# The parameter loads on ScalarE's queue, the skip blocks by one GpSimd selection, and another order of the work

## The chip, the cores and the metric

The kernel runs on one core of a Trainium2 chip. A core has five engines with their own instruction queues: TensorE (PE, matmuls and transposes, with the weight loads PEld beside it), VectorE (DVE), ScalarE (ACT), GpSimd (POOL) and SyncE (SP, which here only issues DMA transfers). Each engine works through its own list in order, and semaphores hold an instruction back until what it reads is written and what it overwrites is read. The metric is the device time of one execution in microseconds (us).

## The reference

Two independent halves over a sequence of S = 2048 rows and D = 1024 columns in bf16, side by side in the output.

- Half A: `kv = shift(k) * v`, where `shift(k)` sums four shifted copies of k, each times a row of `shift_k`; then a long convolution along the sequence with the kernel `ssm_k` (by FFT in the reference), plus `kv * ssm_D`, times q.
- Half B: a diagonal complex state space model. From `Lambda_re`, `Lambda_im` and `log_dt` follow the factors `Lam_bar = exp(dt * Lam)`; then, in each channel p,

```python
Bu = einsum("bld,pd->blp", x, B_bar)
h  = Lam_bar * h + Bu[:, t, :]          # for every t of the sequence
y  = 2 * real(einsum("blp,dp->bld", hseq, Cmat)) + x * Dskip
```

## The kernel before

**How it is staged.** Half B goes through the sequence in 16 chunks of 128 rows. For chunk i, `U.i.jp.jl` (L457) multiplies the transposed x with the transposed matrices BT (16 matmuls of 128 columns each, two for the real and the imaginary part); `ue` evicts the bank to the arena; `r1` and `r2` (L483, L496) rotate by the tables Z1, so that the complex recurrence becomes a real one; `sc` (L502) scans it along the time axis, once for the real and once for the imaginary part; `r3` and `r4` rotate back by Z2; `y` (chunks 0, 1, 2, 14 and 15, L513) or `yq` (the others, in quarters of the array, L526) multiplies by CT and adds the skip term, a matmul of x with the diagonal block `Dd[:, d, :]`; `ye` evicts, and `yst`, `ysp`, `ysg` or `ysh` store. `cy` copies the last state of a chunk to the next.

Half A does its convolution as a transform in two steps: `kvm`, `kva`, `kvb`, `kvc` (L582 to L603) build kv on DVE; `am` and `ae` transform it and `ast` stores it to DRAM; `hl`, `hT`, `hc`, `hm`, `he`, `hst` do the same with `ssm_k`; then for 16 pairs of frequencies `lh`, `lk`, `lw` load both and the constants, `sh` and `sk` do the second step, `she` and `ske` evict, `sw` or `swp` swap rows by DMA, `pr` (L712) multiplies on DVE, `sa`, `sae` and `vst` transform back and store; at the end `vl`, `a3`, `a3e`, `qm` and `ost` or `osp` finish the rows.

**What sets the order.** Everything is written out by hand. The string ORDER (L67) lists 1489 words; each is a task with its arguments, and the letters behind the colon choose arena units (a), PSUM banks (p), scan buffers (h) and weight slots (w). The loop at L773 emits the tasks in that order, so each engine's list is ORDER with the other engines' tasks left out. A tile that reuses an arena unit or a bank waits until its last reader is done. A name with a v at the end (`bcv`, `skev`, `a3ev`) is the same eviction on DVE instead of ACT.

**The start of half B.** `ld_par` (L270) loads five vectors of 1024 numbers into the 40 rows of praw; `par_T` transposes them on PE, `p32` casts them to f32 on DVE; `exp1`, `dve2`, `exp2`, `dve3` make dt, the radius and the angle; `sm_pre`, `tabA1`, `tabA2` reduce angles on DVE (small ones and a table of 1024 columns), `sin0`, `sin1`, `sin2` take the sines on ACT; `par_rest` makes factors from sin0's result; `eo`, `stt`, `z1`, `z2` make the rotation tables Z1 and Z2; `rta` fills the scan's factors. `bl.j.w` loads a block of B, `bT` transposes it on PE (L415), `bc` on ACT or `bcv` on DVE evicts it into BT. `cl`, `cT`, `cc` do the same for C, or `cx` by a transposing DMA. `ld_w`, `wb` and `wbe` load `shift_k`, broadcast it over the partitions by matmuls with a row of ones, and evict it into wbc, which every `kvm` reads whole. `kp` and `vp` load rows of k and v, `x` loads a transposed block of x by DMA.

**The skip blocks.** Dd holds eight diagonal 128x128 blocks with Dskip on the diagonal. `dd` (L365) makes them as eight products of the identity with a column of p32, on DVE (its other form, on ACT, isn't in ORDER).

**Queues.** `spd` (L205) issues on SP, `gpd` (L206) on POOL. SP issues the parameter loads, all loads of B, C, x, k, v, q and the intermediate arrays, `swp`, `ysp`, `ysh`, `osp`; POOL the stores `ast`, `hst`, `vst`, `yst`, `ysg`, `ost`, the swaps `sw` and four small loads. ACT issues no DMA before the change.

Of the kernel before, what the change touches and what calls it, by code (L numbers as in the profile page):

```python
# [67 lines left out]
ld_w:a22 wb.3:p3 ld_par wbe.3:a8 par_T:p4 wb.0:p5 wb.7:p1 p32 ld_F bl.1.0:a39 bl.0.1:a18 wb.5:p7 bl.6.0:a34 bl.4.1:a14  # L68
exp1 dve2 wbe.0 dve3 wb.6:p2 wb.4:p3 wb.2:p0 sm_pre wbe.7 bl.0.0:a27 wbe.5 x.0:a38 wb.1:p7 wbe.6 exp2 kp.1:a0 bl.1.1:a21
kp.0 x.1:a33 bT.0.1:p4 sin0 bc.0.1 wbe.2 tabA1:a47a49a42a12 tabA2 bT.4.1:p5 bl.3.0:a24 bl.5.1:a18 bl.2.1:a51 bl.4.0:a22  # L70
bl.6.1:a41 wbe.1 bT.1.0:p6 sin1 dd wbe.4 bc.1.0 bT.0.0:p1 bl.5.0:a36 sin2 par_rest bc.0.0 bT.6.0:p0 bT.1.1:p6 eo bcv.1.1
bc.4.1 bl.2.0:a28 U.0.0.0:p1 bT.5.1:p3 U.1.0.1:p6 kp.-1 kvm.3:a29 bT.4.0:p7 bc.4.0 U.1.0.0 bT.6.1:p4 bcv.6.0 bT.5.0:p2
bT.2.1:p0 U.0.0.1 bT.3.0:p7 bc.5.0 bc.2.1 bc.5.1 kva.3 kring U.1.2.0:p5 bl.3.1:a23 cl.0.0:a14 bT.2.0:p2 bT.3.1:p0
bl.7.1:a46 ue.1.0:a34 U.0.2.1:p6 bc.3.1 bc.2.0 U.0.2.0 U.1.2.1 cl.3.0:a37 bl.7.0:a26 cl.1.0:a25 bT.7.1:p2 kvb.3:a22
bT.7.0:p0 ue.0.0:a23 bc.6.1 kp.-2 x.3:a21 U.0.1.0:p3 bc.3.0 gz stt cl.2.0:a12 cT.0.0:p4 bc.7.0 bc.7.1 U.0.1.1 U.0.3.0:p0
kvm.1:a15 ue.1.2 vp.1:a27 U.0.3.1 U.3.2.0:p1 ue.0.1 U.3.0.0:p3 z1 kvm.2:a42 z2 ld_Q U.1.1.1:p2 ue.0.2 ue.0.3 x.2:a52
U.1.1.0 cl.3.1:a13 kva.1 cT.1.0:p7 cl.2.1:a32 kva.2 kvb.1:a14 kvb.2:a39 ue.1.1 kvm.0:a15 rta kvc.3 U.3.0.1 cx.6.0 kva.0
cc.1.0 am.3.1:p0p6 cl.1.1:a51 U.3.1.1:p2 ue.3.0:a44 ae.3.0.1:a19 cc.0.0 U.3.2.1 kvc.2 ue.3.2 am.3.0:p7p3 cT.3.1:p0
vp.0:a30 cc.3.1 cx.7.0 kvb.0:a29 U.3.1.0 ue.3.1 cT.1.1:p5 U.3.3.0:p4 r1.0:a46 ae.3.1.1 kvc.0 U.3.3.1 kp.2 am.2.1:p2p0
r2.0:h1 cc.1.1 ue.3.3 cl.0.1:a27 hl.0.1:a23 kvc.1 am.0.0:p5p6 ae.3.0.0 cT.2.1:p1 ae.2.1.1:a40 sc.0.0 hl.0.0 U.1.3.1:p4  # L80
ae.3.1.0 sc.0.1 U.1.3.0 am.0.1:p3p0 ae.0.1.0:a31 cc.2.1 ae.0.0.0 ae.0.0.1 ae.0.1.1 ae.2.0.1 cT.0.1:p7 U.2.0.1:p1
r1.3:a15 cc.0.1 ue.1.3 ast.0 U.2.0.0 am.1.1:p5p3 r3.0:a27 cx.5.0 U.2.3.0:p0 ae.1.0.1:a46 hl.1.0:a48 hl.1.1 ae.1.1.1
am.1.0:p7p6 ae.1.1.0 ae.1.0.0 cT.3.0:p5 cx.4.0 r2.3:h2 cx.5.1 r4.0 cx.7.1 hT.0.1:p4 ue.2.0:a36 cx.4.1 cc.3.0 hT.0.4:p2
cy.1:h0 kvm.4:a14 hT.0.6:p7 hc.0.1:a22 am.2.0:p1p3 r1.1:a27 ae.2.1.0 U.2.3.1 ue.2.3 U.2.2.0:p5 kva.4 hc.0.4:a42 U.2.2.1
cx.6.1 ue.2.2 U.2.1.0:p3 cT.2.0:p2 hc.0.6:a32 cc.2.0 ae.2.0.0 U.2.1.1 ast.3 r2.1 ue.2.1 hT.0.2:p5 hT.0.3:p7 ast.1
hc.0.3:a18 hm.0.6.1:p4p2 hT.0.7:p0 he.0.6.1.1:a43 y.0.0.0:p3 y.0.0.1 hm.0.4.0:p2p6 hdv.0 hc.0.7:a12 he.0.6.1.0
hm.0.7.0:p4p1 hT.0.5:p0 he.0.4.0.1:a29 ast.2 hdv.1 sc.1.0 hT.0.0:p7 he.0.4.0.0 hst.0.4.0 hc.0.2:a20 y.0.0.2
he.0.7.0.0:a50 y.0.0.3 hc.0.0:a13 hm.0.6.0:p4p2 ye.0.0:a19 hm.0.4.1:p5p7 y.0.1.0:p6 y.0.1.1 y.0.1.2 y.0.1.3 vp.2:a34
kvb.4:a31 he.0.6.0.0 sc.1.1 he.0.4.1.1 vp.3:a26 r1.2:a14 he.0.4.1.0 he.0.7.0.1 hst.0.7.0 r3.1:a46 hm.0.0.1:p1p5
hst.0.4.1 hc.0.5:a42 he.0.6.0.1 r4.1 hm.0.0.0:p2p3 he.0.0.1.0:a48 cy.2:h1 r2.2 hm.0.5.1:p7p0 ye.0.1 he.0.5.1.1:a23  # L90
he.0.5.1.0 kp.3 he.0.0.1.1 kvm.6:a38 he.0.0.0.0 y.1.1.0:p4 kvc.4 y.1.1.1 hst.0.6.0 hst.0.6.1 kp.4 kva.6 hst.0.5.1
hm.0.5.0:p6p0 he.0.5.0.0 kvm.5:a14 y.1.1.2 he.0.0.0.1 kvb.6:a25 he.0.5.0.1 y.1.1.3 hm.0.7.1:p2p7 ye.1.1:a28 he.0.7.1.0
kva.5 am.4.0:p1p6 y.1.0.0:p4 he.0.7.1.1 x.4:a32 hm.0.3.0:p2p3 ae.4.0.0:a29 hm.0.3.1:p5p0 hst.0.0.1 hst.0.0.0
he.0.3.1.0:a36 kvc.6 y.1.0.1 he.0.3.1.1 hst.0.5.0 kvb.5:a12 sc.2.1 ae.4.1.0 he.0.3.0.1 kvm.7:a13 y.1.0.2 am.4.1:p1p7
hl.3.0:a40 he.0.3.0.0 hm.0.1.0:p5p0 y.1.0.3 he.0.1.0.0:a38 am.6.1:p5p6 ae.4.1.1 U.4.3.1:p7 he.0.1.0.1 ae.6.0.1:a17
hl.2.1:a44 U.4.3.0 kvc.5 ae.6.1.1 am.6.0:p6p5 U.4.0.0:p2 ae.4.0.1 ue.4.3:a23 U.4.1.1:p3 ae.6.0.0 hm.0.2.0:p0p6 ae.6.1.0
ye.1.0 kva.7 hm.0.1.1:p5p7 sc.2.0 hm.0.2.1:p1p4 hst.0.7.1 hl.3.1 he.0.2.0.0:a34 U.4.1.0 he.0.1.1.0 hl.2.0 he.0.2.1.1
kvb.7:a31 ysp.0 U.4.0.1 r3.2:a48 hT.1.6:p5 he.0.1.1.1 ast.6 ast.4 he.0.2.1.0 hT.1.5:p4 r4.2 he.0.2.0.1 kvc.7 hT.1.4:p6
U.4.2.1:p1 ue.4.1 ue.4.0 hc.1.6:a22 hc.1.4:a19 am.5.1:p7p0 hT.1.3:p2 U.4.2.0 hc.1.5:a33 hT.1.7:p3 am.5.0:p6p4
ae.5.0.1:a15 yst.1 cy.3 y.2.1.0:p7 kp.5 hT.1.1:p5 hst.0.2.0 hd.2 y.2.1.1 ae.5.1.0 hdv.3 ae.5.0.0 hc.1.7:a30 ae.5.1.1  # L100
hst.0.2.1 hT.1.2:p4 y.2.0.0:p6 ue.4.2 hc.1.1:a14 sc.3.1 sc.3.0 hT.1.0:p0 y.2.0.1 am.7.0:p3p1 hc.1.3:a18 hst.0.1.0
r3.3:a40 hm.1.7.1:p5p2 hc.1.0:a34 ae.7.1.0:a27 he.1.7.1.1:a25 hst.0.3.0 y.2.1.2 ae.7.0.0 hst.0.3.1 am.7.1:p2p1 ast.5
y.2.0.2 kvm.8:a48 r4.3 y.2.0.3 he.1.7.1.0 ae.7.0.1 hc.1.2:a31 y.2.1.3 ye.2.0:a47 hm.1.4.1:p4p6 ae.7.1.1 kva.8
hm.1.7.0:p3p5 ye.2.1 yq.3.0:p1p0 hst.0.1.1 he.1.7.0.1 he.1.7.0.0 hm.1.4.0:p7p2 yst.2 he.1.4.1.0:a29 kvm.9:a39 lw.3:w1
kvb.8:a38 he.1.4.0.1 vp.4:a12 yq.3.1 yq.3.2 he.1.4.1.1 he.1.4.0.0 hm.1.3.0:p5p6 he.1.3.0.1:a15 hm.1.3.1:p3p4 he.1.3.1.0
hst.1.7.0 he.1.3.1.1 yq.3.3 hm.1.2.1:p7p6 x.6:a37 he.1.2.1.0:a19 kva.9 he.1.2.1.1 he.1.3.0.0 kvc.8 x.5:a36 lw.1:w2
kvb.9:a35 kvm.10:a47 U.6.1.0:p3 U.6.1.1 am.8.1:p6p7 ast.7 hst.1.7.1 r1.4:a40 kva.10 ae.8.1.1:a44 hst.1.4.1 ae.8.0.1
r2.4:h0 am.8.0:p5p2 ae.8.0.0 ae.8.1.0 hst.1.4.0 ue.6.1:a38 yq.3.4 yq.3.5 hm.1.2.0:p5p7 he.1.2.0.0 x.7:a27 kp.7
hm.1.5.1:p2p6 he.1.5.1.1:a51 he.1.5.1.0 hst.1.5.1 yq.3.6 yq.3.7 ye.3.1:a24 hm.1.5.0:p6p4 kvm.11:a28 he.1.2.0.1 hst.1.2.0
hm.1.0.1:p3p5 cy.4 he.1.5.0.0 kp.6 kvb.10:a33 U.5.1.1:p2 U.5.1.0 sc.4.0 U.6.3.0:p7 kva.11 sc.4.1 hst.1.3.1 ye.3.0  # L110
ue.5.1:a40 he.1.0.1.0:a17 U.5.3.1:p2 hm.1.0.0:p3p1 kvc.9 ast.8 he.1.5.0.1 hst.1.5.0 kvb.11:a46 hm.1.6.0:p0p6 he.1.0.0.0
he.1.0.0.1 he.1.6.0.1:a47 U.5.3.0 hst.1.2.1 hst.1.3.0 U.6.3.1 he.1.6.0.0 U.6.0.1:p1 hm.1.1.0:p6p0 ue.5.3 ysp.3
# [730 lines left out]
```

## Time and profile before

| what | value |
|---|---|
| median of three runs | 343.81 us (343.48 to 343.87) |
| profiled execution, first to last instruction | 343.2 us |
| PE busy | 329.5 us, 96% |
| DVE busy | 325.1 us, 95% |
| ACT busy | 273.5 us, 80% |
| POOL busy | 68.9 us, 20% |
| mean DMA rate over the span | 294 GB/s |
| mean granted TensorE clock | 0.996 |

The profile's own execution has a span of 343.2 us; around the span lies what the runs' times hold besides, so the two are set side by side here. Busy times are unions over an engine's instructions. A matmul's end is modelled, so a busy PE is not a PE at its peak: its records stretch when it has to wait. A DVE or ACT row is a duration, and neighbours in a full queue overlap a little, so that the distance between starts is what one costs. "Idle before" in brackets behind a row is how long the engine had nothing running and what ended that.

### The profile page before, as it was taken

Reading aid. Unit: us, or ns where it says so; the run is one execution under the profiler, and the core shown is the slowest. Engines: PE = TensorE matmul, PEld = TensorE weight load, DVE = VectorE, ACT = ScalarE, POOL = GpSimd, SP = SyncE. Lnnn points to the kernel's source line nnn. Section 1 sums busy time; section 2 is a strip of 40 time slices with the busy share of each in tenths; the row PEclk is TensorE's granted clock in tenths of the full one; section 3 lists DMA queues with packets and bytes.
Section 4 is the critical chain, followed back from the end, with each engine's and each line's share of the span. In section 5 each row is a group of like instructions: output and inputs, shape, how many; then the busy total and the mean of one; then the engine's idle time right before and its main releaser. Section 6 shows DMA issues by size and latency. Waiting matters only on the chain.

```text
span 343.2 us, 11813 instructions
## 1 busy us (share of the span) xinstructions
PE 329.5 (96%) x5086; PEld 230.2 (67%) x5105; DVE 325.1 (95%) x263; ACT 273.5 (80%) x519; POOL 68.9 (20%) x111
## 2 busy tenths in 40 slices
...
GB/s 177 352 351 208 315 281 283 155 318 365 368 269 198 264 263 295 233 261 343 313 353 282 270 339 212 369 272 311 280 314 276 216 326 378 327 335 284 375 346 274
DMA packets 62592, 100.83 MB, mean 294 GB/s; under 512 B 29422, under 2 KB 31614, under 8 KB 62540
## 3 DMA queue, kind: packets, MB, share of 16 engines
...
## 4 chain that ended last, share of the span: by engine, by line
PE 74%; ACT 15%; DMA 4%; issue 3%; DVE 3%; SPq 0%; POOL 0%; DVEq 0%; POOLq 0%
PE bank L464 25%; PE bank L538 19%; PE bank L520 10%; PE bank L754 4%; PE bank L688 4%; PE bank L726 4%; PE bank L608 2%; PE bank L657 2%; ACT BT L431 2%; ACT arena L614 2%; ACT arena L473 2%; ACT CT L439 2%; ACT arena L637 2%; DMA wslot<-a_c_W 1%; DMA arena<-arena 1%
## 5 line engine op out<-in xcount | busy, mean ns | idle before, releaser
L464 PEld LDWEIGHTS <-BT 128*128 128x128 bf16 x2048 | 117.8, 98 | 14.4 <-issue 9.9
L464 PE MATMUL bank<-arena,BT 128*128 128x128 bf16 x2048 | 125.4, 221 | 1.1 <-ACT BT L431 0.9
L538 PE MATMUL bank<-CT,gslot 64*64 64x512 bf16 x1408 | 86.6, 378 | 0.0
L504 DVE TENSOR_TENSOR_SCAN gslot<-rtab,gslot 128x1040 bf16<-128x1040 f32 x32 | 73.0, 2311 | 0.5
L538 PEld LDWEIGHTS <-gslot 64*64 64x64 bf16 x1408 | 36.9, 107 | 30.8 <-issue 1.9
L473 ACT CAST arena<-bank 128x512 bf16<-128x512 f32 x63 | 40.5, 660 | 13.8 <-PE bank L464 13.4
L614 ACT CAST arena<-bank 128x512 bf16<-128x512 f32 x64 | 37.2, 680 | 6.7 <-PE bank L608 4.0
L697 ACT CAST arena<-bank 128x512 bf16<-128x512 f32 x63 | 35.0, 617 | 5.9 <-issue 2.8
L520 PE MATMUL bank<-CT,gslot 128*128 128x512 bf16 x153 | 38.5, 380 | 0.3
L665 ACT CAST arena<-bank 128x512 bf16<-128x512 f32 x64 | 35.2, 631 | 3.1 <-PE bank L657 3.0
L714 DVE TENSOR_TENSOR arena<-arena 128x4096 bf16<-128x4096 bf16 x16 | 36.5, 2280 | 1.1 <-DMA arena<-arena 1.0
L487 DVE TENSOR_TENSOR arena<-gslot,Z 128x4096 bf16<-128x4096 bf16 x16 | 36.6, 2287 | 0.8 <-DVE gslot L504 0.2
L704 ACT CAST arena<-bank 128x512 bf16<-128x512 f32 x60 | 34.4, 621 | 3.2 <-PE bank L688 3.0
L734 ACT CAST arena<-bank 128x512 bf16<-128x512 f32 x60 | 32.4, 616 | 5.5 <-PE bank L726 5.3
L487 DVE TENSOR_TENSOR arena<-arena,Z 128x4096 bf16<-128x4096 bf16 x16 | 36.5, 2280 | 0.1
L556 ACT CAST arena<-bank 128x512 bf16<-128x512 f32 x31 | 18.1, 599 | 16.6 <-PE bank L538 8.7
L588 DVE TENSOR_TENSOR arena<-arena 128x4096 bf16<-128x4096 bf16 (+3 forms) x16 | 30.0, 1881 | 0.0
L668 POOL DMA_DIRECT2D Ys_h<-arena x32 | 23.2, 735 | 25.5 <-ACT arena L665 20.2
L617 POOL DMA_DIRECT2D Ys_kv<-arena x16 | 11.2, 726 | 83.5 <-ACT arena L614 81.1
L520 PEld LDWEIGHTS <-gslot 128*128 128x128 bf16 x160 | 14.1, 98 | 15.9 <-issue 2.3
L688 PE MATMUL bank<-arena,wslot 64*64 64x512 bf16 x256 | 21.5, 382 | 0.3 <-DMA wslot<-a_c_W 0.3
...
## 6 DMA issues: line engine op xcount, KB each, us to landing
...
```

The source lines that it names most:

```text
L464: nc.tensor.matmul(pu[:, w, jl, :], BT[:, 2 * jp + jl, w, d, :], xT[:, d, :], start=(d == 0), stop=(d == ND - 1))
L473: cp(st["u", i][:, :, 2 * jp:2 * jp + 2, :], st.pop(("pu", i, jp)))
L487: nc.vector.tensor_mul(m, s_, win(Z))
L504: nc.vector.tensor_tensor_scan(gf, rtab[:].rearrange("p j t -> p (j t)"), gf, 0.0, ALU.mult, ALU.add)
L520: nc.tensor.matmul(py, h[:, w, j, 2:GW], CT[:, j, w, dh * 512:(dh + 1) * 512], start=(j == 0 and w == 0), stop=False)
L538: mm = nc.tensor.matmul(st["py", i, dh][cols, cs(r)], lhs(dh, rows, c), rhs(dh, rows), start=first, stop=last)
L614: cp(st["ysb", n2][:, p, dh * 512:(dh + 1) * 512], st.pop(("pa", n2, p, dh)))
L665: cp(o, st.pop(("pb", hf, s, e, r)).rearrange("p (n c t) -> p n c t", n=2, c=2))
L688: nc.tensor.matmul(st["ps", nm, g, l][64 * dh:64 * dh + 64, :], st["w", i][rows, a * WC:a * WC + 64], st[nm, i][rows, a, dh * 512:(dh + 1) ...
L697: cp(st["hab", i][:, 0, a, l, :], st.pop(("ps", "h", g, l)))
L704: cp(st["x16", i][:, a, l, :], st.pop(("ps", "k", g, l)))
L714: nc.vector.tensor_mul(hab, st.pop(("x16", i)).rearrange("p a l d -> p (a l d)").unsqueeze(1).to_broadcast([P, 2, 2 * D]), hab)
```

## The change

Three edits. `ld_par` issues its five loads on ScalarE's queue instead of SyncE's. `dd` is one GpSimd selection over all eight blocks: the input is the eight columns of p32, each repeated 128 times along the free axis, and an element is kept where its column number equals its partition number and is 0 elsewhere. ORDER is a new list of the same 1489 tasks, but for the engine of some evictions and the queue of some stores.

```diff
 def ld_par():
     praw = const.tile([5 * NJ, P], BF16, name="praw")
     for pi, ap in enumerate((B_log_dt, B_Lre, B_Lim, B_Dskip, A_ssm_D)):
-        spd(praw[pi * NJ:(pi + 1) * NJ, :], ap.rearrange("(j i) -> j i", i=P))
+        nc.scalar.dma_start(praw[pi * NJ:(pi + 1) * NJ, :], ap.rearrange("(j i) -> j i", i=P))
...
-def dd_(act):
-    for d in range(ND):
-        skip = sm["p32"][:, 3 * NJ + d:3 * NJ + d + 1]
-        if act:
-            nc.scalar.activation(Dd[:, d, :], ident[:], ACT.Copy, scale=skip)
-        else:
-            nc.vector.tensor_scalar(Dd[:, d, :], ident[:], skip, None, ALU.mult)
-E["dd"] = lambda: dd_(False)
-E["dda"] = lambda: dd_(True)
+def dd():
+    skip = sm["p32"][:, 3 * NJ:3 * NJ + ND].unsqueeze(2).to_broadcast([P, ND, P])
+    nc.gpsimd.affine_select(out=Dd[:], in_=skip, pattern=[[0, ND], [-1, P]], compare_op=ALU.is_equal,
+                            fill=0.0, base=0, channel_multiplier=1)
+E["dd"] = dd
```

The lists of the single engines at the start, before (-) and after (+), taken out of ORDER:

```diff
 SP
-ld_par bl.1.0 bl.0.1 bl.6.0 bl.4.1 bl.0.0 x.0 kp.1 bl.1.1 kp.0 x.1 bl.3.0 bl.5.1 bl.2.1 bl.4.0 bl.6.1 bl.5.0 bl.2.0 kp.-1
+bl.1.0 bl.0.1 bl.6.0 bl.4.1 bl.0.0 x.0 kp.1 bl.1.1 kp.0 x.1 bl.3.0 bl.5.1 bl.2.1 bl.4.0 bl.6.1 bl.5.0 bl.2.0 kp.-1
 DVE
-p32 dve2 dve3 sm_pre tabA1 tabA2 dd par_rest bcv.1.1 kvm.3 bcv.6.0 kva.3 kvb.3:a22 stt kvm.1 kvm.2
+p32 dve2 dve3 tabA1 sm_pre tabA2 par_rest bcv.6.0 kvm.3 bcv.4.1 kva.3 bcv.1.1 kvb.3:a15 stt kvm.1 kvm.2
 ACT
-wbe.3 exp1 wbe.0 wbe.7 wbe.5 wbe.6 exp2 sin0 bc.0.1 wbe.2 wbe.1 sin1 wbe.4 bc.1.0 sin2 bc.0.0 eo bc.4.1 bc.4.0
+ld_par exp1 wbe.7 wbe.0 wbe.6 exp2 wbe.3 wbe.5 wbe.4 bc.0.1 bc.0.0 sin1 sin0 bc.1.0 wbe.2 wbe.1 sin2 eo bc.4.0
 PE
-wb.3 par_T wb.0 wb.7 wb.5 wb.6 wb.4 wb.2 wb.1 bT.0.1 bT.4.1 bT.1.0 bT.0.0 bT.6.0 bT.1.1 U.0.0.0
+par_T wb.7 wb.0 wb.6 wb.5 wb.3 wb.4 bT.0.1 bT.0.0 bT.1.0 bT.6.0 wb.2 wb.1 bT.4.1 U.0.0.0
 POOL
-ld_w ld_F kring gz ld_Q rta ast.0 ast.3 ast.1 ast.2 hst.0.4.0
+ld_w gz ld_F kring ld_Q rta ast.0 ast.3 ast.1 dd ast.2 hst.0.4.0
```

In DVE's list later on:

```diff
-r1.2 r3.1 r4.1 r2.2 kvm.6 kvc.4 kva.6
+r1.2 r3.1 kvc.4 r4.1 kvm.6 r2.2 kva.6
...
-r2.9 r1.10 sc.9.0 sc.9.1 r3.9 pr.6 r4.9 pr.8 r2.10
+r2.9 sc.9.1 sc.9.0 r3.9 r4.9 pr.6 r1.10 pr.8 r2.10
```

DVE has 22 evictions before (two of them `bcv`) and 21 after (three `bcv`). PE has the same matmuls; its list behind `yq.8.0` holds the same ones in another order, but for `sh.12` and `sh.13`, which now stand ahead of it. SP stores six whole y blocks (`ysp`) instead of seven, POOL eight (`yst`) instead of seven; of the last two chunks' halves SP stores three (`ysh`) instead of one, POOL one (`ysg`) instead of three; of the rows of half A SP stores five (`osp`) instead of four.

237 lines of the change are left out of this document (119 added, 118 removed).

## The prediction

> **What bounds the kernel now.** I read the stages first: the busy time of each engine between moments that matter to the change. In each row come the stretch (us), its length, then the busy time of PE, weight loads, DVE, ACT and POOL with the number of instructions.
>
> ```profile
> 4.48:20.72 16.24, 14.24 (x118) 11.57 (x118) 14.05 (x36) 16.21 (x35) 1.74 (x6) 1.00 1.09 344
> 20.72:37.95 17.23, 17.23 (x310) 17.16 (x308) 17.23 (x29) 16.43 (x22) 0.00 (x0) 1.00 1.24 275
> 37.95:71.72 33.77, 32.85 (x427) 25.70 (x434) 33.32 (x24) 33.24 (x54) 4.97 (x7) 1.00 0.92 266
> 71.72:208.03 136.31, 135.05 (x2167) 93.52 (x2180) 135.45 (x96) 115.89 (x228) 38.36 (x57) 1.00 0.94 291
> 208.03:325.40 117.37, 116.75 (x2013) 76.15 (x2017) 114.38 (x71) 84.97 (x172) 15.59 (x24) 1.00 0.96 308
> 325.40:343.20 17.80, 12.60 (x66) 5.82 (x63) 10.52 (x11) 5.37 (x10) 4.37 (x7) 0.93 0.86 313
> sum 343.20, PE 329.48 PEld 230.25 DVE 325.14 ACT 273.54 POOL 68.91; mean PE 47.07 PEld 32.89 DVE 46.45 ACT 39.08 POOL 9.84
> ```
>
> From 20.72 to 208 us DVE is idle for 0.45 us in the third row and 0.86 (136.31 - 135.45) in the fourth: it sets the pace, with ACT nearly as full up to 72 us. PE shows as full there too, but a matmul record stretches while PE waits, so that says less. From 208 us to 325.4 us PE is idle for 0.62 us and DVE for 2.99: there PE's work sets the pace, and DVE has slack. The span of this execution is 343.20 us, 0.61 below the 343.81 us median; I carry that 0.61 over.
>
> So a gain must make DVE reach 208 us earlier; what it then spares behind that point is slack. One of its waits in between stands in the list of waits (who waited for whom, us, times, longest):
>
> ```profile
> DVE gslot L498 <- PE bank L523: 0.4, 1, 0.4
> ```
>
> It is r2.2, which wants gslot 1 while the y matmuls of chunk 0 still read it. The other waits stand in brackets in DVE's own start, in order of time:
>
> ```profile
> 4.48 0.20 DVE L284 CAST p<-bank 128x40 f32<-128x40 bf16 x1 [3.48 <-PE bank L279]
> ...
> 6.90 1.17 DVE L320 TENSOR_TENSOR arena<-iot,thn 128x1024 f32<-128x1024 f32 x1
> ...
> 9.97 0.69 DVE L329 TENSOR_SCALAR arena<-arena 128x1024 f32<-128x1024 f32 x1
> ...
> 11.84 1.38 DVE L371 TENSOR_SCALAR Dd<-ident,p 128x128 bf16<-128x128 bf16 x8
> 13.14 0.17 DVE L336 TENSOR_TENSOR lb<-so,r 128x16 f32<-128x16 f32 x1
> ...
> 14.21 0.68 DVE L427 TENSOR_SCALAR BT<-bank 128x1024 bf16<-128x1024 bf16 x1
> 14.81 2.28 DVE L588 TENSOR_TENSOR arena<-arena 128x4096 bf16<-128x4096 bf16 x1
> 17.01 0.68 DVE L429 COPY BT<-bank 128x1024 bf16<-128x1024 bf16 x1
> 17.61 1.21 DVE L595 TENSOR_TENSOR arena<-arena 128x2048 bf16<-128x2048 bf16 x1
> 20.11 0.69 DVE L601 TENSOR_TENSOR arena<-arena 128x1024 bf16<-128x1024 bf16 x1 [1.28 <-PE bank L415]
> 20.72 0.34 DVE L354 SCALAR_TENSOR_TENSOR Z<-arena,b 128x128 bf16<-128x128 f32 x1
> ```
>
> The distance from one start to the next is what an instruction costs in a full queue: the eight products of dd 13.14 - 11.84 = 1.30 us, a BT eviction (bcv) 0.60, the four-block product (kvm) 2.20, a 1024-column sum 0.61. In front is the arrival of the parameters (3.48 us); at 20.11 a sum of the A half (kvb.3) has waited 1.28 us for a transpose (L415) that was still reading its arena unit.
>
> **The change, part by part.** *The five parameter loads.* SP issues them from 0.74 us on, and B's loads stand behind them:
>
> ```profile
> 0.74 0.42 SPq L273 DMA_DIRECT2D praw<-in_B_log_dt_dram  x1
> ...
> 2.23 0.30 SPq L273 DMA_DIRECT2D praw<-in_A_ssm_D_dram  x1
> 2.57 0.37 SPq L420 DMA_DIRECT2D arena<-in_B_B_re_dram  x1
> ```
>
> B's first load moves up by 2.57 - 0.74 = 1.83 us, and everything early on SP's queue with it. ACT starts at 0.73 us too, so the parameters need not land sooner. No row shows what an issue costs ACT. By SP's rows five end at 2.53 us and the table load of 1.28 us behind them at about 3.8, before the first exponential at 4.82: cost nothing. If ACT pays more, or loads its table first (1.28), everything on DVE starts up to 1.3 us later. The other bound is a gain of about 0.5, a broadcast's pace on ACT (4.33 to 4.82, below), since par_T no longer stands behind a broadcast matmul on PE. I take 0, as no row says that the loads had landed by then.
>
> *The order at the start.* tabA1 is moved ahead of sm_pre and tabA2 behind it: the same instructions, so DVE ends tabA2 at 11.84 us as before. dd is gone; par_rest follows, but it reads sin0, which the new order puts late on ACT. ACT's rows:
>
> ```profile
> 4.33 0.58 ACT L408 CAST arena<-bank 128x512 bf16<-128x512 f32 x1 [2.32 <-PE bank L402]
> 4.82 0.21 ACT L287 ACTIVATE dt<-p 128x8 bf16<-128x8 f32 x1
> 5.01 2.05 ACT L408 CAST arena<-bank 128x512 bf16<-128x512 f32 x4
> 6.92 0.24 ACT L293 ACTIVATE r<-a__130 128x8 f32<-128x8 f32 x1
> 7.18 1.28 ACT L314 ACT_TABLE_LOAD   x1
> ```
>
> New on ACT: six wbe from 5.01 us at 0.51 each, to 8.1; exp2, to 8.3; bc.0.1 and bc.0.0 at 0.95 (three took 2.85, below), to 10.2; the table load, to 11.5; sin1 about 1.0 (as many columns as a bc) and sin0 0.2, to 12.7. So par_rest starts at 12.7 us instead of 13.14: of dd's 1.30 us only 0.44 come off here, as ACT is late next. par_rest takes 14.21 - 13.14 = 1.07, to 13.8; bcv.6.0, to 14.4. kvm.3 reads all of wbc, whose last parts (bc.1.0, wbe.2, wbe.1: 0.95 + 2 x 0.51) ACT ends at 14.7, so it starts there, 0.1 before the 14.81 of now. Then 2.20 + 0.60 (bcv.4.1, taken over from ACT) + 1.21 + 0.60 + 0.61 leads to stt at 19.9 us instead of 20.72. The 1.28 us wait is gone, because kvb.3 now writes unit 15, which nothing used; a moved eviction takes 0.60 of it back. **DVE is 0.8 us earlier.**
>
> *Up to r1.0.* The first rotation starts at 37.95 us, where the second row above ends; DVE was full from 20.72 on. It also needs ACT's last ue of chunk 0:
>
> ```profile
> 21.89 2.85 ACT L431 ACTIVATE BT<-bank 128x1024 bf16<-128x1024 bf16 x3 [0.57 <-PE bank L415]
> ...
> 36.12 1.62 ACT L473 CAST arena<-bank 128x512 bf16<-128x512 f32 x3
> ```
>
> ue.0.3 is the second of the three in the last row: done at about 37.2 us. In the new order ACT has as many instructions ahead of this point (36; rta in, one bc out, both near 0.95 us). It loses the 0.49 us from 4.33 to 4.82, in which it evicted a broadcast while the parameters were under way, and may win back the 0.57 us it waited for a transpose, since B's blocks come earlier. So ACT is ready between 37.1 and 37.7 us, DVE at 37.1. I take 37.2: **0.75 gained**, with bounds of 0.25 and 1.2 (the whole 1.28 less what ACT holds).
>
> *r2.2.* In the new order kvc.4 and kvm.6 stand ahead of it (0.6 + 2.2 us of work that was due anyway) while the matmuls it waited for stay where they were in PE's order. The 0.4 us wait is covered: **0.4 gained**. For waits that I don't see in the new order I take 0, between another 1.3 lost (as long as the wait at 20.11) and the 0.86 of idle time left before 208 us gained.
>
> *dd on GpSimd.* The selection stands behind ast.1 on POOL. The nearest rows are the small selection that makes the identity and ast.1's store:
>
> ```profile
> 1.18 0.28 POOL masks.py:199 TENSOR_SCALAR_AFFINE_SELECT ident<-ident 128x128 bf16<-128x128 bf16 x1
> ...
> 53.78 0.69 POOL L617 DMA_DIRECT2D Ys_kv<-arena  x1 [2.43 <-DMA CT<-in_B_C_im_dram]
> ```
>
> Among Dd's readers the first y matmul comes at 62.2 us, and DVE meanwhile runs products of two inputs:
>
> ```profile
> L523 PE MATMUL bank<-Dd,arena x40: 218/219/220, 62.2 to 337.8; 128*128 128x128 bf16 x40
> ```
>
> ```profile
> 55.87 2.28 DVE L487 TENSOR_TENSOR arena<-arena,Z 128x4096 bf16<-128x4096 bf16 x1
> ```
>
> Eight times the columns cost between 0.3 us (if the 0.28 is all overhead) and 8 x 0.28 = 2.3. Behind ast.1 the selection would run from about 54.5 to 57 us, 5 us before the reader at 62.2; only ast.2's store is queued behind it. I take no cost. If it blocks DVE, up to 2.3 us comes on the pace: that is a rival.
>
> *The rest.* The compute order up to chunk 8 has the same DVE work per chunk, apart from neighbours exchanged. Behind it DVE gets two evictions fewer (2 x 0.60), and r4.9 comes 4.4 us of DVE work earlier (r1.10 and pr.6, about 2.2 each, now follow it): slack on an engine that doesn't set the pace there. y stores that change between SP and POOL move no work onto PE or DVE. PE's list behind yq.8.0 has the same matmuls but for sh.12 and sh.13, which now go just ahead of it, so its 117.37 + 17.80 us stay within some tenths.
>
> **Sum:** 0.75 + 0.4, about 1.2 us: span 342.0, time 342.0 + 0.61 = **342.6 us**.
>
> **The rivals.** (1) *Hidden anyway, by ACT.* r1.0 waits for ue.0 until 37.7 and another wait takes r2.2's place: 0.25 gained, 343.5 us. For it: ACT is idle for only 0.03 + 0.80 us between 4.48 and 37.95. Against it: B's loads come 1.83 us earlier. (2) *The search found more.* The 0.86 us of DVE idle before 208 us and the 0.62 of PE behind it go as well: 341.1 us; with r1.0's better bound 340.6. For it: r4.9 is ready longer before PE wants it. Against it: PE's 116.75 us behind 208 remain whatever the order. (3) *GpSimd's selection stops DVE, slower.* Should the selection hold up DVE's products between 54.5 and 57 us for its whole 2.3 us, the sum is 1.2 - 2.3: 344.9 us. It comes out slower from a price of 1.9 us on; at 1 us it only eats the gain. For it: DVE is full there, with two-input products such as the one at 55.87 us. Against it: beside a full DVE, POOL's work now is only DMA issues, and no row shows a DVE product held up. The Trainium skill (SBUF — State Buffer, "Who interferes with whom") states this as a rule: a DVE instruction with two SBUF inputs and a GpSimd instruction that reads SBUF exclude one another, and the second to issue blocks until the first ends. By that rule either DVE waits, as priced here, or the selection does, at no cost with its 5 us in hand; no run here shows which. (4) *The move of the parameter loads doesn't do what it says:* ACT issues them behind its table load or more slowly, all of DVE starts 1.3 us later and the sum is -0.1: 343.9 us.
>
> **How the numbers follow.** A difference under 0.2% (0.69 us) can't be told from none here. Forecast 0.40; (1) 0.21; (2) 0.19; (3) at its full price 0.14; (4) 0.06. Faster by over 0.2% (below 343.1): 0.40 + 0.19 = 0.59. Within 0.2%: 0.21 + 0.06 = 0.27. Slower: 0.14. Likeliest time 342.6; the range goes from (2) at its better bound to (3), 340.6 to 344.9.
>
> **What would show it.** Right: B's first load issued near 0.74 us, stt near 19.9, r1.0 near 37.2, no wait before r2.2, then yq.8.0 near 206.8 us with PE's stretch behind it unchanged in length. Wrong: the first cast of the parameters later than 4.5 us (4); a DVE product beside the selection much longer than 2.3 us, or a gap there (3); DVE idle before r1.0 on an ACT eviction (1); a shorter stretch behind yq.8.0 (2).

## The result, and the profile after

The changed kernel is slower: 349.22 us median of four runs (347.92 to 349.55) against 343.64 us (343.21 to 343.87) for the kernel before on the same chip, a ratio of 1.014 with an interval of 1.0109 to 1.0171. The forecast was 342.6 us, between 340.6 and 344.9: wrong in its sign, and outside its range.

The profiled execution of the changed kernel took 349.0 us and spans 347.3 us. Here are its stages, with the same columns as the rows of the kernel before: stretch, length, busy time of PE, weight loads, DVE, ACT and POOL.

```profile
0.00:6.01 6.01, 0.23 (x2) 0.21 (x3) 0.17 (x2) 1.28 (x1) 5.35 (x16) 1.00 0.64 218
6.01:21.28 15.27, 12.16 (x129) 9.11 (x129) 13.20 (x29) 14.87 (x32) 0.29 (x2) 1.00 1.09 330
...
76.27:212.11 135.84, 133.02 (x2140) 90.98 (x2139) 132.35 (x94) 113.97 (x224) 37.91 (x56) 1.00 0.90 286
212.11:325.80 113.69, 113.17 (x2010) 76.41 (x2008) 110.89 (x65) 83.32 (x170) 15.60 (x24) 1.00 0.93 308
325.80:347.30 21.50, 17.18 (x88) 7.92 (x86) 13.69 (x16) 7.23 (x13) 2.00 (x3) 0.98 0.81 303
```

The cuts are at the same instructions as before: the cast of the parameters (6.01 us, was 4.48), the first stt (21.28, was 20.72), r2.2 (76.27), the end of r4.8 (212.11), which in the kernel before lies within half a us of yq.8.0's start, and a late one. Two things are to be seen. The last two rows add up to 135.19 us; in the kernel before 343.2 - 207.59 = 135.61 us lay behind the end of r4.8. So nothing was lost there. And in the row from 76.27 to 212.11 DVE is idle for 135.84 - 132.35 = 3.49 us; it was 0.86 before. The time was lost ahead of r4.8's end, on DVE. DVE's rows of the changed kernel show where (in brackets the idle time ahead of a row and what ended it):

```profile
6.01 0.20 DVE L285 CAST p<-bank 128x40 f32<-128x40 bf16 x1 [4.94 <-PE bank L280]
...
14.26 0.18 DVE L337 TENSOR_TENSOR lb<-so,r 128x16 f32<-128x16 f32 x1 [1.16 <-ACT so L315]
...
20.68 0.68 DVE L598 TENSOR_TENSOR arena<-arena 128x1024 bf16<-128x1024 bf16 x1
...
38.68 2.29 DVE L484 TENSOR_TENSOR arena<-arena,Z 128x4096 bf16<-128x4096 bf16 x1
...
55.58 2.67 DVE L507 TENSOR_TENSOR gslot<-arena 128x2048 bf16<-128x2048 bf16 x1
...
76.27 1.22 DVE L495 TENSOR_TENSOR gslot<-arena 128x2048 bf16<-128x2048 bf16 x1
...
97.05 2.33 DVE L501 TENSOR_TENSOR_SCAN gslot<-rtab,gslot 128x1040 bf16<-128x1040 f32 x1 [0.31 <-ACT gslot L497]
...
146.08 0.69 DVE L600 TENSOR_TENSOR arena<-arena 128x1024 bf16<-128x1024 bf16 x1 [1.92 <-DMA arena<-in_A_v_dram]
...
201.94 2.32 DVE L501 TENSOR_TENSOR_SCAN gslot<-rtab,gslot 128x1040 bf16<-128x1040 f32 x1 [0.74 <-ACT gslot L497]
...
210.89 1.22 DVE L507 TENSOR_TENSOR gslot<-arena 128x2048 bf16<-128x2048 bf16 x1
```

The last row is r4.8. In the kernel before it stood here:

```profile
206.37 1.22 DVE L510 TENSOR_TENSOR gslot<-arena 128x2048 bf16<-128x2048 bf16 x1
```

So it comes 4.52 us later now, and the span is 4.1 us longer (347.3 against 343.2). In order:

- The parameters land late: the cast is at 6.01 instead of 4.48, and r1.0 (38.68) is 0.73 us later than before instead of 0.75 earlier.
- r4.0 (55.58) takes 2.67 us, where the same form takes 1.22 elsewhere: 1.45 lost, beside the selection.
- r2.2 (76.27) no longer waits: 0.4 won, as forecast.
- A product with v (kvc.13, 146.08) waits 1.92 us for v's rows; two scans wait 0.31 and 0.74 us for the copy of the state (cy) on ACT.

The losses add up to 0.73 + 1.45 + 1.92 + 0.31 + 0.74 - 0.4 = 4.75 us, against 4.52 measured at r4.8.

The 5.6 us between the medians are more than the 4.1 between the spans. The prediction set 0.61 us around the span of the kernel before. In the later runs, which list time and span of each execution, a run stands 1.6 to 2.2 us above its span with every kernel (349.0 against 347.3 here; 344.32 against 342.6 for one run of the kernel before). The time of the execution of the kernel before that was profiled is not on record; by this it took about 343.2 + 1.7 = 344.9 us (an estimate), about 1.1 above its median, so that the two traces show that much less than the medians. Single executions of one kernel lie up to about 2 us from its median and sometimes more; below, a time is judged by its ratio and interval, and a trace by the place where it loses time. The ratios leave out executions that took over 1.5% longer than the fastest of the same kernel (one each of f1 and f3 below, f3's at 855.65 us, and two of the kernel before), which the medians include, so that a ratio is not exactly the quotient of two medians.

### The profile page after: what moved, and what is told of

Its sections match the earlier page's. It is cut to its first block, busy times and chain, and to the rows that moved or that the text cites. A ratio compares the mean times of both kernels' runs of the same rounds, so it can differ in the third digit from the quotient of the medians.

```text
span 347.3 us, 11812 instructions
## 1 busy us (share of the span) xinstructions
PE 328.4 (95%) x5105; PEld 228.4 (66%) x5105; DVE 325.2 (94%) x254; ACT 273.6 (79%) x520; POOL 68.6 (20%) x110
## 4 chain that ended last, share of the span: by engine, by line
PE 47%; DMA 3%; DVE 1%; ACT 1%; issue 0%; SPq 0%; ACTq 0%
PE bank L535 18%; PE bank L461 13%; PE bank L723 4%; PE bank L751 4%; PE bank L517 4%; PE bank L685 4%; DMA arena<-Ys_kv 2%; DVE arena L484 1%; DMA wslot<-a_c_W 1%; ACT arena L731 0%; PE bank L520 0%; ACT arena L694 0%; ACT arena L553 0%; SPq L674 0%; ACTq L553 0%
## 5 line engine op out<-in xcount | busy, mean ns | idle before, releaser
L461 PEld LDWEIGHTS <-BT 128*128 128x128 bf16 x2048 | 116.6, 98 | 18.3 <-issue 12.2
L535 PE MATMUL bank<-CT,gslot 64*64 64x512 bf16 x1408 | 85.2, 377 | 0.3 <-ACT arena L694 0.2
L470 ACT CAST arena<-bank 128x512 bf16<-128x512 f32 x63 | 38.5, 629 | 10.0 <-PE bank L461 7.1
L611 ACT CAST arena<-bank 128x512 bf16<-128x512 f32 x64 | 35.7, 633 | 7.8 <-PE bank L605 4.5
L701 ACT CAST arena<-bank 128x512 bf16<-128x512 f32 x60 | 34.0, 631 | 8.4 <-PE bank L685 7.3
L694 ACT CAST arena<-bank 128x512 bf16<-128x512 f32 x62 | 34.7, 626 | 2.4 <-PE bank L685 2.2
L731 ACT CAST arena<-bank 128x512 bf16<-128x512 f32 x63 | 33.7, 629 | 2.4 <-PE bank L723 2.4
L662 ACT CAST arena<-bank 128x512 bf16<-128x512 f32 x64 | 34.0, 628 | 1.2 <-PE bank L654 1.2
L553 ACT CAST arena<-bank 128x512 bf16<-128x512 f32 x31 | 18.1, 612 | 18.4 <-PE bank L535 10.7
L758 ACT CAST arena<-bank 128x512 bf16<-128x512 f32 x23 | 12.6, 593 | 11.8 <-PE bank L751 11.7
```

The source lines that it names most:

```text
L461: nc.tensor.matmul(pu[:, w, jl, :], BT[:, 2 * jp + jl, w, d, :], xT[:, d, :], start=(d == 0), stop=(d == ND - 1))
L470: cp(st["u", i][:, :, 2 * jp:2 * jp + 2, :], st.pop(("pu", i, jp)))
L535: mm = nc.tensor.matmul(st["py", i, dh][cols, cs(r)], lhs(dh, rows, c), rhs(dh, rows), start=first, stop=last)
L611: cp(st["ysb", n2][:, p, dh * 512:(dh + 1) * 512], st.pop(("pa", n2, p, dh)))
L662: cp(o, st.pop(("pb", hf, s, e, r)).rearrange("p (n c t) -> p n c t", n=2, c=2))
L694: cp(st["hab", i][:, 0, a, l, :], st.pop(("ps", "h", g, l)))
```

## The experiments

| run | kernel | median us | ratio to before (interval) |
|---|---|---|---|
| changed kernel | | 349.22 | 1.0140 (1.0109 to 1.0171) |
| e1_par_on_sp | changed, parameter loads on SP again | 348.15 | 1.0089 (1.0062 to 1.0115) |
| e2_dd_on_dve | changed, skip blocks on DVE again | 349.12 | 1.0124 (1.0069 to 1.0179) |
| e3_both_back | both: the order alone | 348.89 | 1.0109 (1.0051 to 1.0167) |
| e4_par_alone | before, parameter loads on ACT | 346.51 | 1.0061 (1.0035 to 1.0087) |
| e5_v_first | changed, one load of v moved up | 347.66 | 1.0084 (1.0054 to 1.0114) |
| e6_select_twice | changed, two selections | 350.28, one run | |
| e7_b_later | changed, B's loads later | 349.35, one run | |
| e8_order_v_first | e3 with e5 | 347.25 | 1.0082 (1.0052 to 1.0112) |
| f1_select_alone | before, skip blocks by the selection | 344.91 | 1.0017 (0.9997 to 1.0036) |
| f2_repaired | e8, and a copy of the state earlier | 347.52 | 1.0093 (1.0063 to 1.0123) |
| f3_before_plus | before, with three small moves | 344.13 | 0.9996 (0.9978 to 1.0014) |
| g1_all_but_params | f2, parameter loads on ACT | 346.06 | 1.0068 (1.0043 to 1.0092) |

The kernel before stood at 344.31, 344.56, 344.30 and 344.09 us on the chips of the four groups (e1 to e4; e5 to e8; f1 to f3; g1). Where lines are added or left out above them, line numbers shift by a few.

### The parameter loads

**e4_par_alone**, on the kernel before:

```diff
-            spd(praw[pi * NJ:(pi + 1) * NJ, :], ap.rearrange("(j i) -> j i", i=P))
+            nc.scalar.dma_start(praw[pi * NJ:(pi + 1) * NJ, :], ap.rearrange("(j i) -> j i", i=P))
```

> The kernel before with nothing changed but the queue of the five parameter loads: ScalarE instead of SyncE, so that B's loads go out first on SyncE. Theory: the cast of the parameters goes from 4.48 to about 6.0 us, DVE loses about 1.4 us up to chunk 8, and the time outside the span grows from 0.6 to 1.7 us: 343.6 + 1.4 + 1.1 = 346.1 us. Rival (an early delay is taken up by DVE's later waits, and the time outside comes from elsewhere): within 0.7 of 343.6 us.

Its DVE rows: the cast, and the first rotation.

```profile
6.33 0.20 DVE L284 CAST p<-bank 128x40 f32<-128x40 bf16 x1 [5.34 <-PE bank L279]
...
39.03 2.28 DVE L487 TENSOR_TENSOR arena<-arena,Z 128x4096 bf16<-128x4096 bf16 x1
```

The cast is 1.85 us later than in the kernel before, r1.0 1.08 us later, the span 344.3, 1.1 longer. The time rises by 0.61%, 2.1 us. This one line, at a forecast cost of nothing, is a loss by itself. Its time stands 1.9 us above its span, as with the other kernels: the guess that ACT's queue adds time outside the span falls.

**e7_b_later** asks who is slow, ACT's queue or the DMA engines:

```diff
+            spd(pdum[pi * NJ:(pi + 1) * NJ, :], ap.rearrange("(j i) -> j i", i=P))
             nc.scalar.dma_start(praw[pi * NJ:(pi + 1) * NJ, :], ap.rearrange("(j i) -> j i", i=P))
```

> The changed kernel with five more small loads of the same vectors, to a tile that nothing reads, ahead of B's loads on SyncE; the parameters stay on ScalarE's queue at the same times, B's loads go out from 2.6 us instead of 0.8. Theory (the parameters stood behind B's blocks in the DMA engines): the parameters' transpose runs at about 4.0 instead of 5.78 us and the cast at 4.2 to 4.5. Rival (ScalarE's queue itself is slow): the cast stays near 6.0 us.

From its timeline: the last parameter load on ACT's queue, B's first load on SP's, and the transpose and cast of the parameters.

```profile
2.43 0.31 ACTq L276 DMA_DIRECT2D praw<-in_A_ssm_D_dram  x1
...
2.85 0.36 SPq L419 DMA_DIRECT2D arena<-in_B_B_re_dram  x1
...
4.33 0.21 PE L282 MATMUL bank<-ident,praw 40*128 40x40 bf16 x1 [4.33 <-DMA praw<-in_A_ssm_D_dram]
...
4.58 0.20 DVE L287 CAST p<-bank 128x40 f32<-128x40 bf16 x1 [3.52 <-PE bank L282]
```

In the changed kernel the transpose starts at 5.78 us, and by the profile a load of B is the last to end ahead of it:

```profile
5.78 0.19 PE L280 MATMUL bank<-ident,praw 40*128 40x40 bf16 x1 [5.78 <-DMA arena<-in_B_B_im_dram]
```

A load of `shift_k` on GpSimd's queue, issued at 1.63 us in both, bears this out. It takes 3.6 us to land in the changed kernel, and 2.0 in e7 (from the lists of DMA issues, the changed kernel's first):

```profile
arena<-in_A_shift_k_dram POOLq DMA_DIRECT2D x1, 8.0 KB, 3.6
...
arena<-in_A_shift_k_dram POOLq DMA_DIRECT2D x1, 8.0 KB, 2.0
```

The parameters are issued at the same times as in the changed kernel, yet the cast comes at 4.58 us instead of 6.01: it is B's 256 KB blocks, issued from 0.81 us on in the changed kernel, that the small loads stood behind. ACT's queue issues them as fast as SP's did (the last at 2.43 us; on SP at 2.23). The Trainium skill ("DMA: Bandwidth & Descriptors", section "Issuing engines are not separate DMA queues") says that loads of all issuing engines run on the same DMA engines and interleave; this pair of runs agrees, 6.01 against 4.58 us. But the time stays at 349.35 us in its one run: with B's blocks later, ACT's evictions come later too, DVE waits for one of them, and r1.0 starts at 39.86 us, later than the 38.68 of the changed kernel.

**e1_par_on_sp**, the changed kernel with the loads on SP ahead of B's again (e4's diff backwards):

> The changed kernel with its parameter loads issued on SyncE ahead of B's loads again. Theory: they landed late because B's loads of 256 KB were already in the DMA engines; so the cast of the parameters goes from 6.01 back to about 4.5 us, DVE is about 1.4 us earlier up to chunk 8, and the 1.7 us of time outside the span falls to the 0.6 us of the kernel before, if ScalarE's queue is its cause: 349.2 - 1.4 - 1.1 = 346.7 us. Rival (ScalarE holds the start back whatever the loads do, and the time outside the span has another cause): the cast is early, but the first rotation stays near 38.7 us and the time within 0.5 of 349.2 us.

```profile
3.03 2.65 POOL L392 MEMSET arena<- 1x3072 bf16 x1
4.15 0.20 DVE L285 CAST p<-bank 128x40 f32<-128x40 bf16 x1 [3.09 <-PE bank L280]
...
4.63 1.08 DVE L291 CAST dt<-dt 128x8 f32<-128x8 bf16 x1 [0.28 <-ACT dt L288]
...
14.41 0.18 DVE L337 TENSOR_TENSOR lb<-so,r 128x16 f32<-128x16 f32 x1 [2.25 <-ACT so L315]
```

The cast comes at 4.15 us, as the theory had it; but what follows gives it back. The next cast, eight columns, takes 1.08 us instead of 0.17: it ends as GpSimd's memset of the key ring ends (3.03 + 2.65 = 5.68). Then par_rest waits 2.25 us for the sine on ACT, which itself had waited 1.90 us for a transpose of B:

```profile
10.79 1.02 ACT L428 ACTIVATE BT<-bank 128x1024 bf16<-128x1024 bf16 x1 [1.90 <-PE bank L412]
```

So r1.0 starts at 38.82 us, no earlier than in the changed kernel. That is the rival's case. The ratio fell all the same, by half a per cent, to the number that the theory had forecast (346.7 over 343.6 is 1.009); in the profiled execution the waits of 0.31 us at 97.05 and of 0.74 us at 201.94 are missing. What brought the time down isn't settled by it.

### The selection

**e6_select_twice** issues the same selection a second time.

```diff
         nc.gpsimd.affine_select(out=Dd[:], in_=skip, pattern=[[0, ND], [-1, P]], compare_op=ALU.is_equal,
                                 fill=0.0, base=0, channel_multiplier=1)
+        nc.gpsimd.affine_select(out=Dd[:], in_=skip, pattern=[[0, ND], [-1, P]], compare_op=ALU.is_equal,
+                                fill=0.0, base=0, channel_multiplier=1)
```

> The changed kernel with the selection issued twice in a row on GpSimd (same output). Theory (the selection keeps DVE's two-input sum r4.0 from running for as long as it lasts): r4.0 grows from 2.67 by about another 1.2 us to 3.9, or a second DVE instruction behind it grows by that much; the first rotation r1.1 starts at about 60.5 instead of 59.30 us. Rival (r4.0 was long for another reason): r4.0 stays at 2.7 us and r1.1 at 59.3.

First the timeline of the changed kernel at that place, then that of the run with two:

```profile
55.93 1.23 POOL L368 TENSOR_SCALAR_AFFINE_SELECT Dd<-p 128x1024 bf16<-128x1024 f32 x1
...
58.17 1.21 DVE L592 TENSOR_TENSOR arena<-arena 128x2048 bf16<-128x2048 bf16 x1
...
59.30 2.28 DVE L484 TENSOR_TENSOR arena<-arena,Z 128x4096 bf16<-128x4096 bf16 x1
```

```profile
56.03 2.67 DVE L509 TENSOR_TENSOR gslot<-arena 128x2048 bf16<-128x2048 bf16 x1
56.39 1.23 POOL L368 TENSOR_SCALAR_AFFINE_SELECT Dd<-p 128x1024 bf16<-128x1024 f32 x1
57.69 1.97 POOL L370 TENSOR_SCALAR_AFFINE_SELECT Dd<-p 128x1024 bf16<-128x1024 f32 x1
58.62 2.10 DVE L594 TENSOR_TENSOR arena<-arena 128x2048 bf16<-128x2048 bf16 x1
...
60.65 2.28 DVE L486 TENSOR_TENSOR arena<-arena,Z 128x4096 bf16<-128x4096 bf16 x1
```

With one selection, r4.0 takes 2.67 us and ends 1.1 us after the selection does (57.16 us): it hardly ran until then. With two, r4.0 is as long. The second selection, which begins before r4.0 ends (57.69 against 58.70 us), takes 1.97 us instead of 1.23, and the next sum takes 2.10 us instead of 1.21; r1.1 starts at 60.65 instead of 59.30 us, of which 0.45 is r4.0's later start (56.03 against 55.58). DVE's two-input products stand still while GpSimd selects, and a selection that comes in between waits for a product. The Trainium skill ("SBUF — State Buffer", section "Who interferes with whom") has it that of a DVE instruction with two SBUF inputs and a GpSimd instruction that reads SBUF the second to issue blocks. Both runs agree that the two exclude one another, with 1.45 and about 2.3 us lost on DVE (1.45 + 2.10 - 1.21). Who has to wait can't be read from which record begins first: r4.0's begins 0.35 us ahead of the selection's (55.58 and 55.93), and yet it was r4.0 that waited.

**e2_dd_on_dve** puts the eight products back on DVE, with `dd` ahead of `par_rest` in ORDER.

```diff
-        nc.gpsimd.affine_select(out=Dd[:], in_=skip, pattern=[[0, ND], [-1, P]], compare_op=ALU.is_equal,
-                                fill=0.0, base=0, channel_multiplier=1)
+        for d in range(ND):
+            skip = sm["p32"][:, 3 * NJ + d:3 * NJ + d + 1]
+            nc.vector.tensor_scalar(Dd[:, d, :], ident[:], skip, None, ALU.mult)
```

> The changed kernel with the skip blocks as eight DVE products ahead of par_rest, where DVE waits 1.16 us for a sine; no GpSimd selection. Theory (the selection stopped DVE): the product r4.0 takes 1.22 us instead of 2.67, the products cost 1.30 - 1.16 = 0.14: 349.2 - 1.45 + 0.14 = 347.9 us. Rival (r4.0's record is long for another reason, or the loss is covered later): r4.0 stays above 2 us or the time stays at 349.2 to 349.4 us.

```profile
55.77 1.22 DVE L507 TENSOR_TENSOR gslot<-arena 128x2048 bf16<-128x2048 bf16 x1
...
180.46 2.29 DVE L711 TENSOR_TENSOR arena<-arena 128x4096 bf16<-128x4096 bf16 x1 [2.46 <-DMA arena<-arena]
```

r4.0 is back at 1.22 us, and r1.5 starts at 152.79 instead of 154.25 us. But in this execution a later product (pr) waited 2.46 us for swapped rows, and r4.8 came at 211.13 us, no earlier than before the repair. The median moved by 0.1 us, the ratio by less than its uncertainty: the cause of the long r4.0 is shown, a gain in time isn't.

**f1_select_alone** makes the edit of the changed kernel alone on the kernel before (the last diff backwards), and moves one word:

```diff
-... sin1 dd wbe.4 ... ast.1 hc.0.3:a18 ...
+... sin1 wbe.4 ... ast.1 dd hc.0.3:a18 ...
```

> The kernel before with one thing changed: the skip blocks by one GpSimd selection, behind ast.1 on GpSimd as in the changed kernel, instead of eight DVE products. Theory (the selection stops DVE, and the 1.30 us of products that it saves early is lost in the wait for a transpose at 20.11 us): stt stays near 20.7 us, kvb.3's wait grows from 1.28 to about 2.5 us, a two-input DVE instruction beside the selection is about 1.3 us longer, and the time is 343.8 + 1.3 = 345.1 us, ratio 1.004. Rival (the products were worth their 1.30 us): ratio 0.996 to 1.000.

```profile
36.95 2.29 DVE L483 TENSOR_TENSOR arena<-arena,Z 128x4096 bf16<-128x4096 bf16 x1
...
53.37 7.02 POOL L367 TENSOR_SCALAR_AFFINE_SELECT Dd<-p 128x1024 bf16<-128x1024 f32 x1
...
58.20 1.23 DVE L494 TENSOR_TENSOR gslot<-arena 128x2048 bf16<-128x2048 bf16 x1
59.34 1.14 DVE L643 TENSOR_TENSOR arena<-arena,p 128x2 bf16<-128x2 bf16 x2
```

Neither theory had it. The products' time wasn't swallowed by the wait for the transpose: r1.0 starts at 36.95, 1.0 us earlier. And here the selection is the one that waits: 7.02 us, until DVE's row of large products ends at 59.34 us; then it holds up two tiny products of 2 columns, which take 1.14 us. A us won and most of a us lost: 1.0017, no difference that can be measured. The profiled execution, with 343.25 us, was the fastest of its ten.

### The order's own waits

**e5_v_first** moves one word of ORDER:

```diff
-... vp.7:a21 x.10:a23 ae.11.0.1 kva.13 kvm.15:a12 kvb.13:a33 kva.12 vp.6:a30 kvc.13 ...
+... vp.6:a30 vp.7:a21 x.10:a23 ae.11.0.1 kva.13 kvm.15:a12 kvb.13:a33 kva.12 kvc.13 ...
```

SP's queue in the changed kernel, and its entry in the list of waits (who for whom, us, times, longest): vp.5 is issued at 117.47 us, vp.7 behind it waits until 137 us for a store of `ssm_k`'s transform (Ys_h) that still reads its unit, and only then come a block of x and vp.6.

```profile
117.47 19.66 SPq L576 DMA_DIRECT2D arena<-in_A_v_dram  x2
137.22 1.90 SPq L444 DMA_TRANSPOSE arena<-in_B_x_dram  x1
139.21 0.53 SPq L576 DMA_DIRECT2D arena<-in_A_v_dram  x1
```

```profile
SPq L576 <- DMA Ys_h<-arena: 18.7, 1, 18.7
```

> The changed kernel with one word of the order moved: the load vp.6 ahead of vp.7 on SyncE's queue, where vp.7 waits until 137.1 us for a store that still reads its unit. Theory (v's rows are late only because vp.6 stands behind that wait): kvc.13 starts about 1.9 us earlier (144.2 instead of 146.08) with no wait, r1.5 at 152.4 instead of 154.25, and the time falls from 349.2 to about 347.4 us. Rival (another load or PE's own pace ends last there): the wait turns up again at kvc.15 or kvc.12, or the time stays within 0.5 of 349.2 us.

```profile
144.90 0.69 DVE L600 TENSOR_TENSOR arena<-arena 128x1024 bf16<-128x1024 bf16 x1
...
153.05 2.29 DVE L484 TENSOR_TENSOR arena<-arena,Z 128x4096 bf16<-128x4096 bf16 x1
```

The product with v has no wait left, r1.5 starts 1.2 us earlier although this execution began 0.5 us later (r1.0 at 39.19), and the ratio falls from 1.0140 to 1.0084, which is worth 1.9 us, as expected, and just clear of the uncertainty. The largest single loss was a load queued behind another's wait. The kernel before has vp.7 ahead of vp.6 as well; there vp.7 waits 6.6 us for such a store, and no product on DVE waits for v.

**e3_both_back** and **e8_order_v_first** try the order alone: the changed kernel with the parameter loads as in e1 and the products as in e2, e8 with the move of e5 besides.

> The changed kernel's order with both edits of code undone: parameter loads on SyncE first, skip blocks on DVE ahead of par_rest. Theory (three additive losses, the third being the order's own late loads of v near 146 us and two waits for the state copies): 349.2 - 2.5 - 1.0 = 345.7 us, still 2 us above the kernel before, with the wait of 1.9 us near 144 us still there. Rival (the order is as good as before, and the late loads of v came only from the shift of the start): 343.2 to 343.6 us, no wait there.

> The changed kernel's order alone (parameter loads on SyncE first, skip blocks on DVE ahead of par_rest) with vp.6 ahead of vp.7. Theory: without the late v loads (1.5 us of DVE in that run) the order's DVE is as early as in the kernel before up to r1.5; the other losses of the order (pr.1 waiting for its rows, the stretch from 250 us on) stay: 348.9 - 1.5 = 347.4 us, ratio to before about 1.007. Rival (the late stretch takes back whatever is gained early): ratio stays at 1.011.

e3 still has its wait for v (1.5 us) and comes out at 1.0109, above what three additive losses would leave (1.006 by its own expectation, 345.7 over 343.6), though 1.006 lies inside its interval. e8 gives 1.0082, near its expectation; its interval takes in the rival's 1.011 too. Its profiled execution, with 350.40 us the longest of its ten, lost 3.85 us to a wait that is 1.0 us or less in the others, the scan of chunk 3 waiting for the copy of the state:

```profile
99.07 4.54 DVE L498 TENSOR_TENSOR_SCAN gslot<-rtab,gslot 128x1040 bf16<-128x1040 f32 x2 [3.85 <-ACT gslot L494]
```

DVE has one small sum to do (kvc.7, 0.6 us) between r4.2, which makes the state, and the scan. In the new order hc.1.6 and two small products stand ahead of cy.3 on ACT, and in the changed kernel cy.3 starts 0.63 us after r4.2's end (96.77 against 96.14); in the kernel before it starts 0.09 us after it (94.69 against 94.60), and the scan doesn't wait. In e8's execution ACT had waited 2.15 us for a store at 86.85 us and 2.06 us for matmuls at 92.43, and cy.3 came at 98.78. That this delay became DVE's wait through the thin margin is likely, but no run tried it apart.

**f2_repaired** is e8 with cy.3 moved up, and **g1_all_but_params** is f2 with the parameters on ACT behind B's loads. Both have:

```diff
-... hT.1.6:p6 hc.1.6:a33 hd.2 hT.1.4:p0 r4.2 cy.3 ...
+... hT.1.6:p6 r4.2 cy.3 hc.1.6:a33 hd.2 hT.1.4:p0 ...
```

> The changed kernel's order with all four losses mended: parameter loads on SyncE first, skip blocks on DVE ahead of par_rest, vp.6 ahead of vp.7, and r4.2 and cy.3 moved ahead of hc.1.6, so that ScalarE copies the state as soon as r4.2 ends. Theory (these four are the loss): no wait before sc.3 and kvc.13, DVE at r4.8 no later than in the kernel before, time within 1 us of it, ratio 0.999 to 1.003. Rival (the order has a loss of its own behind 208 us, where loads of Ys_kv and of weights end last): ratio stays near 1.008.

> The changed kernel with three losses mended and the parameters left on ScalarE behind B's loads: skip blocks on DVE ahead of par_rest, vp.6 ahead of vp.7, r4.2 and cy.3 ahead of hc.1.6. It differs from the repaired order, whose ratio to the kernel before was 1.0093, only in the queue of the parameter loads. Theory (the start is a trade: this order wants B's blocks early, so with the parameters first its transposes wait longer for B, and moving the parameters back gained nothing): time as in the repaired order or shorter, ratio 1.005 to 1.009. Rival (losses add up; late parameters cost 1.4 us here as well): ratio about 1.013.

PE at the start of f2, then of g1, and r4.8 on DVE in g1:

```profile
3.78 0.19 PE L277 MATMUL bank<-ident,praw 40*128 40x40 bf16 x1 [3.78 <-DMA praw<-in_A_ssm_D_dram]
...
10.18 2.74 PE L409 MATMUL bank<-ident,arena 128*128 128x128 bf16 x24 [2.58 <-DMA arena<-in_B_B_re_dram]
```

```profile
5.71 0.19 PE L277 MATMUL bank<-ident,praw 40*128 40x40 bf16 x1 [5.71 <-DMA arena<-in_B_B_im_dram]
```

```profile
207.03 1.23 DVE L504 TENSOR_TENSOR gslot<-arena 128x2048 bf16<-128x2048 bf16 x1
```

f2's theory fails. The waits ahead of kvc.13 and sc.3 are gone, yet r4.8 comes at 208.60 us, 2.23 later than in the kernel before: 1.33 of it is lost at r1.0 already (39.28 us), and a sum waits 1.36 us at 110.78 for matmuls. The rival has the ratio right but not the place: behind r4.8 there are 135.47 us, as before.

With the parameters first, PE has them at 3.78 us but then waits 2.58 us for B; with B first it waits until 5.71 for the parameters. Giving the parameters their place back gains nothing in this order (1.0093 against 1.0068; the intervals overlap): the start is a trade. In g1's trace DVE reaches r4.8 at 207.03 us instead of 210.89, and the span is 343.7 us. Its r4.8 is 0.66 us later than in the kernel before, and r1.0 0.65 (38.60 against 37.95): what it still loses up to there, it loses at the start. The 0.68% left in its time is near the 0.61% that e4 measured for the moved loads, but as f2 is no faster with the loads moved back, it isn't shown to be the same loss.

**f3_before_plus** takes the good parts to the kernel before, and clears the key ring earlier on GpSimd:

```diff
-... ld_F ... kp.1:a0 ... kring ... kvb.3:a22 ... r4.1 ... r2.2 ... kvm.6:a38 ... kvc.4 ...
+... kring:a0 ld_F ... kp.1 ... kvb.3:a40 ... kvc.4 r4.1 ... kvm.6:a38 r2.2 ...
```

> The kernel before with three small moves, two of them the good ones of the new order: kvb.3 writes an arena unit that nothing used, kvc.4 and kvm.6 go ahead of r2.2, and GpSimd clears the key ring ahead of its F1t load, so that it is done before the parameters come. Theory: the waits of 1.28 us at 20.11 and of 0.4 us at 71.7 are gone, the cast of dt takes 0.17 instead of 0.39 us; r1.0 comes 0.25 to 1.2 us earlier (ScalarE's ue.0 bounds it), r4.8 0.6 to 1.6 us earlier, time 342.3 to 343.2 us, ratio 0.996 to 0.998. Rival (what DVE gains early is lost to loads later, as in the repaired order): ratio 0.999 to 1.001.

```profile
36.44 2.29 DVE L485 TENSOR_TENSOR arena<-arena,Z 128x4096 bf16<-128x4096 bf16 x1
...
204.93 1.23 DVE L508 TENSOR_TENSOR gslot<-arena 128x2048 bf16<-128x2048 bf16 x1
```

r1.0 is 1.5 us and r4.8 1.44 us earlier than in the profiled execution of the kernel before, and the span is 341.8; yet the medians differ by 0.17 us and the ratio's interval excludes a gain above 0.22%. Part of the difference is that the profiled execution of the kernel before was one of its longer ones, as worked out above; where the rest goes in the others stays open. No version here beats the kernel before.

## Why the prediction was wrong, step by step

- **DVE's arrival at r4.8 sets the end, PE's stretch behind it is fixed: right.** The time from r4.8's end to the end of the span was 135.61 us before and 135.19 after, and lies between 134.5 (e7) and 136.4 us (e3) in all fourteen traces. To within about 1 us, what was lost ahead of it was carried to the end.
- **"Cost nothing" for the five parameter loads: wrong, and the first step that failed.** The sum looked at ACT's issues, which did go as forecast, and at B's loads coming 1.83 us earlier only as a gain. The cost was that B's blocks now fill the DMA engines ahead of the small loads (e7): the cast is 1.53 us later, above the bound of 1.3. Rival (4) had nearly that price, with another cause. Behind the cast the working held in the changed kernel: cast to stt was forecast at 19.9 - 4.48 = 15.4 us and took 21.28 - 6.01 = 15.27, with the sine late on ACT and kvb.3's wait gone, as it said. So r1.0 came at 38.68 instead of 37.2. That it held is in part luck. B's blocks had come by then because they had gone ahead of the parameters; where the same order has the parameters early, at 4.15 us in e1 and at 4.00 in f2, ACT waits 1.90 and 2.52 us for transposes of B, and cast to stt takes 17.27 and 17.89 us. The forecast counted on early parameters and on early blocks of B at once. No run has both, and r1.0 lies between 38.17 (e3) and 39.86 us (e7) in all ten traces with the new order.
- **r2.2's wait covered, 0.4 gained: right.**
- **"For waits that I don't see I take 0": wrong, the largest term.** They are 1.92 + 0.31 + 0.74 = 2.97 us, more than twice the bound of 1.3. e5 shows the largest: SP's list was followed for the start only, and a load that waits for its unit held up the loads behind it for about 20 us. The bound came from one wait of the old order, which says little about a list of 1489 tasks newly arranged.
- **The selection at no cost: wrong; rival (3) is what happened.** It took 1.23 us, inside the 0.3 to 2.3 given, and cost DVE 1.45 us (e2, e6). The rule that was quoted left open who would wait; in the changed kernel DVE did, in f1 mostly the selection. "No row shows a DVE product held up" was true of products, but the kernel before had a sign of it: its cast of dt takes 0.39 us at 5.06 us, where the changed kernel's takes 0.17, and ends as GpSimd's memset ends (2.77 + 2.65 = 5.42).
- **Only 0.44 of the products' 1.30 us come off at the start, as ACT is late next: right.** From the cast to par_rest it was 8.66 us before, 8.22 in the forecast and 14.26 - 6.01 = 8.25 after, and par_rest waited for the sine on ACT. The same luck with B's blocks goes into it.

The sum, -1.15 us forecast against +4.52 at r4.8, is thus off by 1.48 (the start, with the parameters) + 1.45 (selection) + 2.97 (waits) = 5.90 us, against 5.67 seen. The slow end of the range, 344.9 us, priced rival (3) alone; here three losses came together.

In the ratios, v's load is worth 0.56% (1.0140 to 1.0084). The selection and the late copy of the state together are worth 0.16% (1.0084 to 1.0068), inside the uncertainty. The remaining 0.68% isn't traced to a single cause: in g1's trace it is lost at the start, but neither place of the parameter loads mends it. That the losses add up is only roughly so: e1, e3 and e8 each mended something and stayed between 1.008 and 1.011.
